# Sigmoid attention and a spatially gated MLP on one core: the 64-row tail of the spatial product as row tiles of two batches, with four accumulators open together

## Chip, cores, metric

One core of one Trainium2 chip. The metric is the device time of one execution in microseconds (us); the kernel before took 665.77 us (median of 3 runs, 665.56 to 666.07). Below, PE is TensorE's matmul stream, PEld its weight loads, DVE is VectorE, ACT ScalarE, POOL GpSimd, SP the queue that issues most DMAs.

## The reference, cut to what matters

```python
# q, k, v: (8 batches, 12 heads, 448 tokens, 64); all fp32
attn = sigmoid(q @ k.T / 8 - log(448)); x = (attn @ v) as (8, 448, 768)
h = relu(x @ w_in)                      # 768 -> 1024
u, v = h[..., :512], h[..., 512:]
v_n = (v - mean(v)) / sqrt(var(v) + 1e-6)
v_s = einsum('ts,bsd->btd', w_spatial, v_n) + b_spatial   # the spatial product, 448 x 448
out = (u * v_s) @ w_out                 # 512 -> 768
```

## The kernel before, in words

Batches are worked in four rounds of two (`m` = 0 to 3; an even batch `b0`, an odd one `b1`). A round is `attention(m)`, then `gate_values` for seven token tiles in groups (0,1), (2,3), (4,5), (6), then the spatial products, the gating by `u` and the output products, in an order that is written out by hand at the end of `attn_gmlp_kernel` (L690 to L713). `in_program_order` ties every engine to that order: whatever stands first in an engine's program waits first.

**Two-part numbers.** fp32 operands are split into a high and a low part in the type fp32r. `product` (L376) issues for each chunk of the contraction three matmuls, high-high, low-high and high-low (`TERMS`), all into one bank of PSUM.

**The spatial product.** 448 tokens are three chunks of 128 rows and a tail of 64. For one batch and one of four feature blocks `fc` of 128, `spatial` (L451) issues 3 x 3 matmuls for the full chunks and two for the tail: 11 of 448 columns, 352 in the whole kernel. The tails of both batches share the tile `vns[3]` ("the short tile"), whose two halves are filled so that `[:, 0]` holds the even batch's high part in rows 0 to 63 and its low part in rows 64 to 127, and `[:, 1]` the odd batch's low part in rows 0 to 63 and its high part in rows 64 to 127. The spatial weights of the tail stand in both halves of the rows. So the first tail matmul (times the weights' high part, 128 rows) gives high-high plus low-high at once, and the second (times the weights' low part, also 128 rows) gives high-low, and low-low with it.

**PSUM.** One pool `ps_2` of four buffers, each two banks, which is all of PSUM, serves every product (`banks`, L115): `pv` (gate values, L379 by way of `product`), `pg` (spatial), `pu` (the `u` half), `po` (output), `psc` and `pav` (attention). A new tile takes a buffer when the reader of that buffer's last tile is done. The four groups of `gate_values` fill all four just before the spatial products; their readers are the `relu` on ACT (L414).

**Round 0 also loads weights.** `load_weights(n)` runs n steps of a generator that splits `w_in` and `w_out`: DVE (L126, L129, L132, L199, L215), ACT (L200, L205), SP (L158). `gate_values` calls it ahead of its `relu`, `spatial` (2 steps) ahead of the bias addition (L473), `gated` 2 steps ahead of L496 and 2 at its end. In rounds 1 to 3 the generator is empty.

**After the spatial products.** `spatial` ends with the DVE addition of the bias (L473) into a tile `g` of the three-buffer tag `tmp`. `gated` (L478) forms `pu`, multiplies (L496), and splits the result (L109 on ACT, L110 on DVE) for `output` (L512), which needs both halves of a batch. `start_loads(m + 1)` puts the next round's loads on SP.

Order of the products in a round: `pg` of b0 (two groups of two `fc`), `pu` of b0 (two), `pg` of b1 (two), `po` of b0 for the first third, `pu` of b1 (two), the rest of `po`.

Of the kernel before, what the change touches and what calls it, by code (L numbers as in the profile page):

```python
# [14 lines left out]
P = 128  # L15
# [20 lines left out]
def attn_gmlp_kernel(  # L36
# [25 lines left out]
    nc = tc.nc  # L62
    B, NHP, _, _ = qk.shape
    S = out.shape[3]
# [5 lines left out]
    HALF = 64  # L70
    NFULL = 3
# [24 lines left out]
    w_sp_s = const.tile([P, 4, 2, 512], F32R, name="w_sp_s")  # L96
    b_bc = const.tile([P, 512], F32, name="b_bc")
# [10 lines left out]
    def split(hi, lo, src, copy):  # L108
        copy(hi, src)  # L109
        nc.vector.tensor_sub(lo, src, hi.bitcast(F32))  # L110

    def banks(name):
        return ps_2.tile([P, 2, 512], F32, tag="ps2", name=name)
# [112 lines left out]
    def load_weights(n):  # L226
        for _ in range(n):
            next(weights, None)
# [22 lines left out]
    def attention_splits(b, hp, halfway=False):  # L251
        raw = loaded[b, hp][:, HALF:]
        s = work.tile([P, 2, 2 * S], F32R, tag="split", name=f"qks_{b}_{hp}", bufs=3)[:, :, :PART]
        (nc.vector.tensor_copy if b > 1 or halfway else nc.scalar.copy)(s[:, 0], raw)  # L254
        parts_of[b, hp] = s
        if not halfway:
            finish_splits(b, hp)
# [12 lines left out]
    TERMS = ((0, 0), (1, 0), (0, 1))  # L270
# [104 lines left out]
    def product(ps, pairs, more=()):  # L375

        ops = [(st(a), mv(c)) for st, mv in pairs for a, c in TERMS] + list(more)
        for i, (st, mv) in enumerate(ops):
            nc.tensor.matmul(ps, st, mv, start=i == 0, stop=i == len(ops) - 1)  # L379
# [10 lines left out]
    def half_of(w, o, k, n):  # L390

        block, col = divmod((o // 2 * n + k) * 2 + o % 2, 4)
        return w[:, block, :, col * P : (col + 1) * P]

    vns = {}
# [50 lines left out]
    def cols_of(b):  # L446
        return slice(0, S) if b % 2 else slice(512 - S, 512)

    gates = {}

    def spatial(b, fcs):  # L451

        odd = b % 2
        cols = cols_of(b)
        pg = banks(f"pg_{b}_{fcs[0]}")
        for i, fc in enumerate(fcs):
            fs = slice(fc * P, (fc + 1) * P)
            pairs = []
            for c in range(NFULL):
                vn = vns[c + 4 if odd else c]  # L460
                pairs.append(
                    (lambda a, vn=vn: vn[:, a, fs], lambda p, c=c: w_sp_s[:, c, p, cols])
                )

            short = vns[NFULL][:, odd, fs]
            product(
                pg[:, i, :S], pairs, [(short, w_sp_s[:, NFULL, a, cols]) for a in range(2)]
            )
        load_weights(2)
        g = work.tile([P, 2, 512], F32, tag="tmp", name=f"g_{b}_{fcs[0]}", bufs=3)[:, :, :S]  # L470
        bb = b_bc[:, cols]
        bb = bass.AP(bb.tensor, bb.offset, [list(bb.ap[0]), [0, 2], list(bb.ap[1])])
        nc.vector.tensor_add(g, pg[:, :, :S], bb)  # L473
        gates[b, fcs] = g

    hidden = {}
# [1 line left out]
    def gated(b, fcs):  # L478

        odd = b % 2  # L480
        g = gates.pop((b, fcs))
        pu = banks(f"pu_{b}_{fcs[0]}")
        for i, fc in enumerate(fcs):
            fs = slice(fc * P, (fc + 1) * P)
            product(
                pu[:, i, :S],
                [
                    (
                        lambda a, cc=cc: half_of(w_u[0], fc, cc, NCC)[:, a],
                        lambda c, cc=cc: x_s[:, c, cc, odd * S : (odd + 1) * S],  # L490
                    )
                    for cc in range(NCC)
                ],
            )
        load_weights(2)
        nc.vector.scalar_tensor_tensor(g, pu[:, :, :S], 0.0, g, op0=ALU.max, op1=ALU.mult)  # L496
        if odd:
            gs = [
                work.tile([P, 2, 512], F32R, tag="big", name=f"gs_{b}_{fcs[0]}_{a}", bufs=BIG)[:, :, :S]
                for a in range(2)  # L500
            ]
        else:
            gs = work.tile([P, 2, 2 * S], F32R, tag="split", name=f"gs_{b}_{fcs[0]}", bufs=3)
            gs = [gs[:, a].rearrange("p (i s) -> p i s", i=2) for a in range(2)]
        split(gs[0], gs[1], g, nc.scalar.copy)
        for i, fc in enumerate(fcs):
            hidden[b, fc] = [part[:, i] for part in gs]
        load_weights(2)

    def output(b, es, final=False):  # L510

        osb = work.tile([P, 2, 512], F32, tag="tmp", name=f"osb_{b}_{es[0]}", bufs=3)[:, :, :S]  # L512
        if final:

            pos = [banks(f"po_{b}_{e}")[:, 0, :S] for e in es]
        else:
            po = banks(f"po_{b}_{es[0]}")
            pos = [po[:, i, :S] for i in range(2)]
        for i, e in enumerate(es):
            product(  # L520
                pos[i],
                [
                    (
                        lambda a, fc=fc: half_of(w_out_s, e, fc, NFC)[:, a],
                        lambda c, fc=fc: hidden[b, fc][c],
                    )
                    for fc in range(NFC)
                ],
            )
            if final:  # L530
                h = S // 2
                nc.scalar.copy(osb[:, i], pos[i])  # L532
                nc.sync.dma_start(out[b, e, :, h:], osb[:, i, h:])
                nc.scalar.dma_start(out[b, e, :, :h], osb[:, i, :h])
        if final:
            return
        nc.scalar.copy(osb, po[:, :, :S])  # L537
        nc.sync.dma_start(out[b, es[0] : es[0] + 2].rearrange("e p s -> p e s"), osb)
# [7 lines left out]
    def start_loads(m):  # L546
        n = m * 2 * NHP
        ahead(attention_loads, n)
        ahead(attention_loads, n + 1)
        ahead(value_loads, n)  # L550
        ahead(attention_loads, n + 2)
        ahead(attention_loads, n + 3)
        if m:
            ahead(value_loads, n + 2)
# [85 lines left out]
    def attention(m):  # L640

        if m:
            attention_by_fours(m)
            return
        end = 2 * NHP
        ats = {}

        def scores(n, ts):
            for t in ts:
                ats[n, t] = attention_scores(*units[n], t)  # L650

        short, evens, odds = (NFULL,), tuple(range(NFULL)), tuple(range(NFULL + 1, TILES))
        full = evens + odds
        for n in (0, 2):
            if not n:
                first_splits(*units[0])
            if n:
                scores(n, short + evens)
            else:
                scores(n, evens)  # L660

            def loads():
                ahead(value_loads, n + 2, end)
                ahead(attention_loads, n + 4, end)
                ahead(attention_loads, n + 5, end)

            if n:
                loads()
            scores(n, odds)
            if not n:  # L670
                scores(n, short)
            for t in full:
                if copied(*units[n], t):
                    sigmoid(ats[n, t], ats[n, t])
            if not n:
                loads()
            load_weights(3 if n else 2)
            for i in range(3 if n else 2):
                attention_splits(*units[n + 2 + i])
            if not n:  # L680
                load_weights(1)
            attention_values(*units[n], lambda t: ats.pop((n, t)), direct=n)
        attention_by_fours(0)
        w_u.append(const.tile([P, NCC, 2, F], F32R, tag="w_u", name="w_u_s"))
# [4 lines left out]
    pairs = [(0, 1), (2, 3)]  # L689
    for m in range(B // 2):  # L690
        attention(m)
        for ts in ((0, 1), (2, 3), (4, 5), (6,)):
            gate_values(m, ts)
        b0, b1 = 2 * m, 2 * m + 1
        more = m < B // 2 - 1
        for fcs in pairs:
            spatial(b0, fcs)
        for fcs in pairs:
            gated(b0, fcs)
        for fcs in pairs:  # L700
            spatial(b1, fcs)
        start_loads(m + 1)
        output(b0, (0, 1))
        for fcs in pairs:
            gated(b1, fcs)
        output(b0, (2, 3))
        output(b0, (4, 5))
        if more:
            for n in range(3):
                attention_splits(*units[(m + 1) * 2 * NHP + n])  # L710
        output(b1, (0, 1))
        output(b1, (2, 3))
        output(b1, (4, 5), final=not more)  # L713
# [55 lines left out]
```

## Time and profile before

| | |
|---|---|
| median of 3 runs | 665.77 us (665.56 to 666.07) |
| profiled execution: its own time, its span | 666.02 us, 664.2 us |
| PE busy | 659.2 us, 99% of the span, 3830 matmuls |
| DVE, ACT, POOL busy | 318.0, 250.1, 18.5 us |
| granted TensorE clock, mean | 1.0 |

How to read it: busy shares say how much an engine worked, the view of waits says which engine stood still and for whom, the chain says what followed what up to the end, and the timeline gives start and length of each run of like instructions. The end of a matmul is modelled, so rates are taken from starts, not from lengths.

### The profile page before, as it was taken

What the parts mean: (1) busy time and instruction counts of PE and PEld (TensorE: products, weight loads), DVE (VectorE), ACT (ScalarE), POOL (GpSimd) and SP (SyncE); (2) the same over time, 40 slices, a digit from 0 to 9 for tenths busy, and PEclk for the clock granted to TensorE, in tenths of its full rate; (3) what the DMA queues carried; (4) which work ended last, traced back from release to release, by engine and by line L of the source; (5) the groups of instructions that cost most, each with busy time, mean ns of one, the idle gap of its engine ahead of it and who ended that gap; (6) DMA issues with size and microseconds to landing.
All of it is one profiled execution on the core that took longest, in us unless ns stands there. A gap on an engine that the chain in (4) does not pass through costs nothing.

```text
span 664.2 us, 8979 instructions
## 1 busy us (share of the span) xinstructions
PE 659.2 (99%) x3830; PEld 510.1 (77%) x3830; DVE 318.0 (48%) x464; ACT 250.1 (38%) x283; POOL 18.5 (3%) x36
## 2 busy tenths in 40 slices
PE   9999999999999999999999999999999999999997
PEld 3655889999765588999966558899986655899997
DVE  4989888852545237223156515721315741653110
ACT  5986322411766510011187641010127872101011
POOL 0000010000000002000000001100000000110000
PEclk9999999999999999999999999999999999999999
DMA  8755213432431310000344050000024510000003
GB/s 298 238 179 188 63 37 94 136 122 83 169 140 58 137 60 0 1 29 0 112 141 169 29 178 18 1 1 28 29 84 142 169 56 1 1 1 0 29 29 111
DMA packets 20695, 55.75 MB, mean 84 GB/s; under 512 B 1968, under 2 KB 8496, under 8 KB 20656
## 3 DMA queue, kind: packets, MB, share of 16 engines
q1 hardware_dynamic: 20368, 54.96, 24.2%
q8 instruction: 30, 0.49, 0.3%
q10 hardware_dynamic: 288, 0.23, 0.1%
q14 instruction: 9, 0.07, 0.0%
HBM read 44.17 MB, written 11.01 MB: 83 GB/s over the span
## 4 chain that ended last, share of the span: by engine, by line
PE 99%; ACT 0%; DVE 0%; issue 0%
PE pav L346 20%; PE pu L379 17%; PE po L379 17%; PE pv L379 17%; PE psc L311 14%; PE pg L379 11%; PE psc L293 3%; PE warm L388 0%; ACT osb L532 0%; DVE zeros L384 0%; DVE bias_s L100 0%; DVE mhalf L102 0%
## 5 line engine op out<-in xcount | busy, mean ns | idle before, releaser
L275 ACT ACTIVATE at<-psc,bias_s 128x896 f32<-128x896 f32 x129 | 120.4, 1009 | 6.1 <-PE psc L311 4.6
L346 PE MATMUL pav<-at,v 128*64 128x448 f32 (+1 forms) x684 | 120.1, 544 | 0.0
L379 PE MATMUL pu<-x_s,w_u_s 128*128 128x448 f32 x576 | 116.5, 362 | 0.0
L379 PE MATMUL po<-gs,w_out_s 128*128 128x448 f32 x576 | 116.5, 362 | 0.0
L379 PE MATMUL pv<-w_g_s,x_s 128*128 128x512 f32 x504 | 115.4, 390 | 0.0
L379 PEld LDWEIGHTS pu<-x_s,w_u_s 128*128 128x128 f32 x576 | 108.0, 188 | 7.2
L379 PEld LDWEIGHTS po<-gs,w_out_s 128*128 128x128 f32 x576 | 108.0, 187 | 7.3
L379 PEld LDWEIGHTS pv<-w_g_s,x_s 128*128 128x128 f32 x504 | 94.3, 188 | 22.3 <-PE pav L346 2.8
L346 PEld LDWEIGHTS pav<-at,v 128*64 128x64 f32 (+1 forms) x684 | 41.7, 136 | 70.8 <-issue 64.0
L311 PEld LDWEIGHTS psc<-qks 64*128 64x128 f32 x840 | 77.9, 185 | 14.8 <-DVE x_s L110 5.2
L311 PE MATMUL psc<-qks 64*128 64x448 f32 x840 | 88.6, 365 | 0.0
L379 PE MATMUL pg<-w_sp_s,vn 128*128 128x448 f32 x352 | 71.7, 362 | 0.0
L379 PEld LDWEIGHTS pg<-w_sp_s,vn 128*128 128x128 f32 x352 | 66.0, 187 | 4.7
L109 ACT CAST gs<-g 128x896 fp32r<-128x896 f32 x16 | 15.1, 942 | 120.3 <-DVE g L496 120.3
L537 ACT COPY osb<-po 128x896 f32<-128x896 f32 x23 | 20.9, 908 | 104.1 <-PE po L379 104.1
L110 DVE TENSOR_TENSOR x_s<-pav,x_s 128x896 fp32r<-128x896 f32 x16 | 17.1, 1089 | 81.5 <-ACT x_s L109 81.5
L496 DVE SCALAR_TENSOR_TENSOR g<-pu,g 128x896 f32<-128x896 f32 x16 | 17.5, 1091 | 80.1 <-PE pu L379 80.1
L261 DVE TENSOR_TENSOR qks<-raw,qks 128x848 fp32r<-128x848 f32 x46 | 47.4, 1039 | 1.1 <-ACT qks L254 0.2
L414 ACT ACTIVATE rv<-pv 128x1024 f32<-128x1024 f32 (+1 forms) x16 | 14.7, 919 | 75.9 <-PE pv L379 75.9
L418 DVE BATCH_NORM_STATS2 stats<-rv 128x6 f32<-128x512 f32 x28 | 19.0, 679 | 38.9 <-ACT rv L414 38.9
L109 ACT CAST x_s<-pav 128x896 fp32r<-128x896 f32 x16 | 14.1, 909 | 53.9 <-PE pav L346 53.9
L591 DVE COPY wval_s<-psc 128x896 f32<-128x896 f32 x9 | 9.8, 1092 | 47.3 <-PE psc L311 47.3
(59 smaller groups left out, 368.7 us busy)
## 6 DMA issues: line engine op xcount, KB each, us to landing
raw<-qk_dram SPq DMA_DIRECT2D x47, 456.0 KB, 5.1
v<-v_dram SPq DMA_DIRECT2D x24, 448.0 KB, 3.6
out_dram<-osb SPq DMA_DIRECT2D x23, 448.0 KB, 2.6
wraw<-w_in_dram SPq DMA_DIRECT2D x12, 512.0 KB, 6.2
wraw<-w_out_dram SPq DMA_DIRECT2D x6, 512.0 KB, 3.4
wraw<-w_sp_dram SPq DMA_DIRECT2D x4, 256.0 KB, 6.2
raw<-qk_dram SPq DMA_DIRECT2D x1, 296.0 KB, 2.9
b_bc<-b_sp_dram SPq DMA_DIRECT2D x1, 256.0 KB, 6.6
```

Source lines behind the costliest of these rows:

```text
L109: copy(hi, src)
L110: nc.vector.tensor_sub(lo, src, hi.bitcast(F32))
L261: nc.vector.tensor_sub(s[:, 1], loaded[b, hp][:, HALF:], s[:, 0].bitcast(F32))
L275: nc.scalar.activation(at, src, AF.Sigmoid, bias=bias_s, scale=QK)
L293: nc.tensor.matmul(psc[odd * HALF : (odd + 1) * HALF, j, :S], raw[rows, :HALF], raw[rows, HALF + Q :], start=True, stop=True,)
L311: nc.tensor.matmul(psc[:, j, :S], st[rows, k : k + P], mv[rows, Q:PART], start=i == 0, stop=i == len(ops) - 1,)
L346: nc.tensor.matmul(pav[heads, odd, :S], vt[rows, t, heads], at[rows, j], start=start, stop=t == NFULL,)
L379: nc.tensor.matmul(ps, st, mv, start=i == 0, stop=i == len(ops) - 1)
L414: nc.scalar.activation(rv[:, :n], pv[:, :n], AF.Relu)
L418: nc.vector.bn_stats(stats, rv[:, i])
L496: nc.vector.scalar_tensor_tensor(g, pu[:, :, :S], 0.0, g, op0=ALU.max, op1=ALU.mult)
L537: nc.scalar.copy(osb, po[:, :, :S])
```

## The change

The eight spatial accumulators of a round (two batches, four `fc`, in four two-bank tiles) are opened together. The second tail matmul of each is replaced by one on 64 rows alone, which holds the high part, so that high-low is formed and low-low no longer; the even batch's uses rows 0 to 63 and the odd batch's rows 64 to 127, and the two are issued one behind the other into different banks. All eight of a round stand in `spatial_shorts`, behind the first `spatial` group. The order of the round becomes: `pg` b0 first half, the eight short ones, `pg` b0 second half, `pg` b1 (two), `pu` b0 (two), `pu` b1 first, `start_loads`, `po` b0 first third, `pu` b1 second, the rest of `po`. The bias additions are issued after their accumulators end; that of the last tile stands behind `gated(b0, ...)`'s first group.

```diff
+    def spatial_room(b, fcs):
+        pgs[b, fcs] = banks(f"pg_{b}_{fcs[0]}")
+    def spatial_shorts(m, groups):
+        for fcs in groups:
+            for i, fc in enumerate(fcs):
+                for odd in range(2):
+                    b = 2 * m + odd
+                    rows = slice(odd * HALF, (odd + 1) * HALF)
+                    nc.tensor.matmul(
+                        pgs[b, fcs][:, i, :S],
+                        vns[NFULL][rows, odd, fc * P : (fc + 1) * P],
+                        w_sp_s[rows, NFULL, 1, cols_of(b)],
+                        start=(b, fcs) not in begun,
+                        stop=(b, fcs) in begun,
+                    )
+            begun.update((2 * m + odd, fcs) for odd in range(2))
...
     def spatial(b, fcs):
-        pg = banks(f"pg_{b}_{fcs[0]}")
+        pg = pgs[b, fcs]
...
-            product(
-                pg[:, i, :S], pairs, [(short, w_sp_s[:, NFULL, a, cols]) for a in range(2)]
-            )
+            ops.append((vns[NFULL][:, b % 2, fs], w_sp_s[:, NFULL, 0, cols]))
+            ended = (b, fcs) in begun
+            for n, (st, mv) in enumerate(ops):
+                nc.tensor.matmul(pg[:, i, :S], st, mv,
+                    start=n == 0 and not ended, stop=n == len(ops) - 1 and ended)
+        begun.add((b, fcs))
         load_weights(2)
+    def biased(b, fcs):
...
-        nc.vector.tensor_add(g, pg[:, :, :S], bb)
+        nc.vector.tensor_add(g, pgs.pop((b, fcs))[:, :, :S], bb)
...
-        for fcs in pairs:
-            spatial(b0, fcs)
-        for fcs in pairs:
-            gated(b0, fcs)
-        for fcs in pairs:
-            spatial(b1, fcs)
+        for b in (b0, b1):
+            for fcs in pairs:
+                spatial_room(b, fcs)
+                if (b, fcs) == (b0, pairs[0]):
+                    spatial(b, fcs)
+        spatial_shorts(m, pairs)
+        biased(b0, pairs[0])
+        for b, fcs in ((b0, pairs[1]), (b1, pairs[0])):
+            spatial(b, fcs)
+            biased(b, fcs)
+        spatial(b1, pairs[1])
+        gated(b0, pairs[0])
+        biased(b1, pairs[1])
+        gated(b0, pairs[1])
+        gated(b1, pairs[0])
         start_loads(m + 1)
         output(b0, (0, 1))
-        for fcs in pairs:
-            gated(b1, fcs)
+        gated(b1, pairs[1])
```

## Rows read from the trace of the kernel before

**Rows 1.** The profile's page, two lines: busy time by engine (us, share of the span, instructions), and the chain that ended last, by engine.

```profile
PE 659.2 (99%) x3830; PEld 510.1 (77%) x3830; DVE 318.0 (48%) x464; ACT 250.1 (38%) x283; POOL 18.5 (3%) x36
PE 99%; ACT 0%; DVE 0%; issue 0%
```

**Rows 2.** The view of waits, PE alone: who waited for whom, total us, times, longest.

```profile
PE warm L388 <- DVE zeros L384: 1.2, 1, 1.2
```

**Rows 3.** The chain in order of time (start us, us, what): the spatial products, the `u` products and the next ones of round 0, and a block of 36 score pairs of round 2.

```profile
95.07 8.81 PE pg L379 x44
103.88 14.41 PE pu L379 x72
...
335.37 7.40 PE psc L311 x72
```

**Rows 4.** Timeline of PE, one row from each of four short stretches at 335 us (start us, us, what, count): the last four-tile matmuls of 64x64, then the first pairs of 64-row matmuls (64*128 is rows times columns of the stationary).

```profile
334.82 0.56 PE L293 MATMUL psc<-raw 64*64 64x448 f32 x4
335.30 0.47 PE L311 MATMUL psc<-qks 64*128 64x448 f32 x2
335.62 0.56 PE L311 MATMUL psc<-qks 64*128 64x448 f32 x4
335.82 0.56 PE L311 MATMUL psc<-qks 64*128 64x448 f32 x4
```

**Rows 5.** The same view at 333 us: a 128-row output product is followed by 64x64 tiles.

```profile
333.15 0.56 PE L379 MATMUL po<-gs,w_out_s 128*128 128x448 f32 x2
333.35 0.36 PE L379 MATMUL po<-gs,w_out_s 128*128 128x448 f32 x1
333.64 0.61 PE L293 MATMUL psc<-raw 64*64 64x448 f32 x4
334.06 0.56 PE L293 MATMUL psc<-raw 64*64 64x448 f32 x4
```

**Rows 6.** The same view at 342 us: 64-row pairs are followed by pairs of 128 rows and 64 columns.

```profile
342.42 0.36 PE L311 MATMUL psc<-qks 64*128 64x448 f32 x2
342.71 0.60 PE L346 MATMUL pav<-at,v 128*64 128x448 f32 x2
343.13 0.92 PE L346 MATMUL pav<-at,v 128*64 128x448 f32 x4
```

**Rows 7.** The same view at 392 us: 64x64 tiles are followed by full 128x128 matmuls.

```profile
392.57 0.54 PE L346 MATMUL pav<-at,v 64*64 64x448 f32 x2
393.04 0.50 PE L379 MATMUL pv<-w_g_s,x_s 128*128 128x512 f32 x1
393.38 0.63 PE L379 MATMUL pv<-w_g_s,x_s 128*128 128x512 f32 x2
393.61 0.62 PE L379 MATMUL pv<-w_g_s,x_s 128*128 128x512 f32 x2
```

**Rows 8.** Timeline of round 0 around the start of the spatial products, PE, then ACT, then one DVE row (brackets: idle before, and releaser).

```profile
94.91 8.97 PE L379 MATMUL pg<-w_sp_s,vn 128*128 128x448 f32 x44
...
98.31 0.62 ACT L205 CAST w_u_s<-wval_s 128x512 fp32r<-128x512 f32 x1 [3.87 <-DVE wval_s L132]
101.54 0.68 ACT L200 ACTIVATE wraw<-wraw 128x512 f32<-128x512 f32 x1 [2.60 <-DVE wraw L199]
102.11 0.59 ACT L414 ACTIVATE rv<-pv 128x512 f32<-128x512 f32 x1
...
101.02 0.43 DVE L199 TENSOR_SCALAR wraw<-wraw 128x512 f32<-128x512 f32 x1
```

**Rows 9.** The chain at the start of the kernel: the step from a DVE memset to the first matmul that waited for it.

```profile
0.91 0.28 DVE zeros L384
1.19 0.05 issue
```

**Rows 10.** Timeline of round 1: PE's spatial products, and the same `relu` on ACT.

```profile
258.32 8.97 PE L379 MATMUL pg<-w_sp_s,vn 128*128 128x448 f32 x44
...
258.57 0.60 ACT L414 ACTIVATE rv<-pv 128x512 f32<-128x512 f32 x1 [3.10 <-PE pv L379]
```

**Rows 11.** Timeline of DVE: the last write of token tile 6 (L436) in round 0 and in round 1.

```profile
105.47 0.75 DVE L436 SCALAR_TENSOR_TENSOR vn<-rv,rstd,vn 128x512 fp32r<-128x512 f32 x1
...
263.68 0.75 DVE L436 SCALAR_TENSOR_TENSOR vn<-rv,rstd,vn 128x512 fp32r<-128x512 f32 x1
```

**Rows 12.** Timeline of DVE in round 0 behind that: weight steps (first rows of two runs of them), bias additions, the gating and its split.

```profile
106.13 0.69 DVE L129 SCALAR_TENSOR_TENSOR wval_s<-wraw,wval_s 128x512 uint32<-128x512 uint32 x1
...
108.86 1.09 DVE L473 TENSOR_TENSOR g<-pg,b_bc 128x896 f32<-128x896 f32 x1
109.86 0.68 DVE L129 SCALAR_TENSOR_TENSOR wval_s<-wraw,wval_s 128x512 uint32<-128x512 uint32 x1
...
112.59 1.09 DVE L473 TENSOR_TENSOR g<-pg,b_bc 128x896 f32<-128x896 f32 x1
...
116.31 1.08 DVE L496 SCALAR_TENSOR_TENSOR g<-pu,g 128x896 f32<-128x896 f32 x1
118.40 1.09 DVE L110 TENSOR_TENSOR gs<-g,gs 128x896 fp32r<-128x896 f32 x1 [1.01 <-ACT gs L109]
119.41 0.69 DVE L129 SCALAR_TENSOR_TENSOR wval_s<-wraw,wval_s 128x512 uint32<-128x512 uint32 x1
```

**Rows 13.** Timeline of SP in round 0: the next round's loads, then the outputs.

```profile
123.64 6.15 SPq L241 DMA_DIRECT2D raw<-qk_dram  x2
...
137.31 34.37 SPq L538 DMA_DIRECT2D out_dram<-osb  x6
```

**Rows 14.** Timeline of PE at the start: the first matmuls of 512 columns, and the first two pairs of 64 rows that follow one another at the later rate.

```profile
1.23 2.74 PE L388 MATMUL warm<-zeros 128*128 128x512 bf16 x6 [1.23 <-DVE zeros L384]
...
5.94 0.66 PE L311 MATMUL psc<-qks 64*128 64x448 f32 x4
```

More of the change, by code (lines that the diff above doesn't have):

```diff
@@ L449, in attn_gmlp_kernel @@
     gates = {}
+    pgs = {}
+    def spatial_room(b, fcs):
[14 more added lines that the diff above has]
+            begun.update((2 * m + odd, fcs) for odd in range(2))
@@ L451, in spatial @@
+    begun = set()
     def spatial(b, fcs):
-        odd = b % 2
         cols = cols_of(b)
-        pg = banks(f"pg_{b}_{fcs[0]}")
+        pg = pgs[b, fcs]
         for i, fc in enumerate(fcs):
             fs = slice(fc * P, (fc + 1) * P)
[L458 to L462, printed above, removed]
-                )
-            short = vns[NFULL][:, odd, fs]
-            product(
-                pg[:, i, :S], pairs, [(short, w_sp_s[:, NFULL, a, cols]) for a in range(2)]
-            )
+            ops = [
+                (vns[c + 4 if b % 2 else c][:, a, fs], w_sp_s[:, c, p, cols])
+                for c in range(NFULL)
+                for a, p in TERMS
+            ]
+            ops.append((vns[NFULL][:, b % 2, fs], w_sp_s[:, NFULL, 0, cols]))
+            ended = (b, fcs) in begun
+            for n, (st, mv) in enumerate(ops):
+                nc.tensor.matmul(
+                    pg[:, i, :S],
+                    st,
+                    mv,
+                    start=n == 0 and not ended,
+                    stop=n == len(ops) - 1 and ended,
+                )
+        begun.add((b, fcs))
@@ L469, in spatial @@
         load_weights(2)
+    def biased(b, fcs):
         g = work.tile([P, 2, 512], F32, tag="tmp", name=f"g_{b}_{fcs[0]}", bufs=3)[:, :, :S]
-        bb = b_bc[:, cols]
+        bb = b_bc[:, cols_of(b)]
         bb = bass.AP(bb.tensor, bb.offset, [list(bb.ap[0]), [0, 2], list(bb.ap[1])])
-        nc.vector.tensor_add(g, pg[:, :, :S], bb)
+        nc.vector.tensor_add(g, pgs.pop((b, fcs))[:, :, :S], bb)
         gates[b, fcs] = g
```

## The prediction

> **What bounds the kernel now.** The page comes first: PE is busy for 659.2 of 664.2 us and is 99% of the chain that ended last [rows 1]. The view of waits comes second: PE waits once in the whole execution, 1.2 us at the start [rows 2]. So every TensorE slot that goes is time won, and every wait that PE is given is time lost, with nothing downstream to absorb it. Third come rates, from the chain and from starts in the timeline: 44 spatial matmuls in 8.81 us and 72 of `u` in 14.41 us make 0.200 us for one of 448 columns [rows 3].
>
> **Part 1: slots removed.** A round has eight high-low tail matmuls, 8 x 0.200 = 1.60 us. Now each has 64 rows, and two run at once if they lie in different row halves and banks. The attention scores have that very shape: successive pairs start at 335.62 and 335.82, so a pair takes one slot of 0.20 [rows 4]. Four pairs are 0.80 us; 0.80 us a round is saved, 3.2 us in four rounds.
>
> **Part 2: two changes of tile shape a round.** The short pairs stand between full 128x128 matmuls, so PE goes to 64-row tiles and back, 8 times in all. The trace has neither change, but both their ends, in starts:
> - Leaving 128x128 for 64x64: 333.35 to 333.64 is 0.29 where a slot is 0.20, so 0.09 lost [rows 5].
> - The first 64x128 pair after another shape holds up the second: 335.30 to 335.62 is 0.32 against 0.20, so 0.12 (two decimals; over the block, 7.40 us for 36 pairs is 0.20 above 36 x 0.200, both losses together [rows 3, 4]).
> - Leaving 64x128: 342.42 to 342.71 is 0.29, again 0.09; the 64-column shape behind it loses less at its second start, 0.42 (342.71 to 343.13) where the steady step of such tiles is 0.38 (two of them from 334.06 to 334.82), so 0.04 to 0.05 [rows 4 to 6].
> - Entering 128x128: 393.04 to 393.38 is 0.34 where the next step is 0.23, so 0.11 [rows 7].
>
> In: 0.09 + 0.11 = 0.20. Out: 0.09 + 0.11 = 0.20. I take 0.40 us a round, 1.6 us in all; the nearest rows bound a change by 0.14 (rows 5 and 6 with their cheaper second halves) and 0.22, so 1.1 to 1.8 us. Parts 1 and 2 leave a saving of 3.2 - 1.6 = 1.6 us (1.4 to 2.1).
>
> The Trainium skill, page "TensorEngine Tiling (Array Packing)", section "Key Properties", says that a change of tiling mode, unlike a change of tile, drains the engine. The rows agree, with 0.20 us for each. A sum that follows the same page's section "Theoretical Speedup" alone, up to twice for a contraction of 64, would keep all of the 3.2 us.
>
> **Part 3: the wait for the fourth accumulator, round 0.** The pool has four buffers, and the short pairs of the second group need all four, so one is the buffer of the last gate product (token tile 6), free only when its `relu` on ACT is done. Before, the first two spatial tiles took older buffers and this one was needed from 103.7 on. In round 0 that `relu` is late: on ACT it stands behind a weight step (L200, 101.54), which waits for DVE (L199, 101.02), and runs from 102.11 to 102.70 [rows 8]. Nothing in front of it is touched by the change. PE's new times: the first spatial group starts at 94.91 and has 20 matmuls, so it ends at 98.91; pairs start at 99.00 and 99.32; the even half of the third at 99.52; its odd half, which is the first to write the fourth buffer, waits until 102.70 plus about 0.05 for the hand-over (0.05 of issue between a DVE memset and its matmul [rows 9]), 102.75. The refilled array again spends some 0.31 to the last pair (the 0.20 + 0.11 above), 103.06, and 0.30 to the first full matmul, 103.36. Without the wait that would be 99.72 + 0.30 = 100.02. Cost: 3.3 us. Bounds: 3.2 (nothing but the delay from 99.52 to 102.75) and 3.7 (if the fourth buffer falls to the first pair and all four come after 102.75).
>
> Behind PE's waiting matmul stands all of its program; DVE and ACT go on. In rounds 1 to 3 there are no weight steps: the `relu` starts 0.25 us after the first spatial matmul and ends at 259.17, while the third pair would come about 4.6 us after 258.32, at 262.9 [rows 10]. No wait there.
>
> **Part 4: what moved.** The odd batch's spatial products follow the even batch's directly, so token tile 6 is needed earlier. Round 0: the second group runs 103.36 to 107.5, and tile 6 is wanted at the seventh matmul of the next, 108.7; DVE wrote it by 106.22 [rows 11]: covered by 2.5 us, but only because PE waited before. Round 1: wanted at 268.7, there at 264.43. Zero.
>
> Round 0's DVE queue is nearly gapless behind this: two weight steps take 2.73 us (106.13 to 108.86), a bias addition 1.0, gating 1.08, the wait for ACT 1.01, the split 1.0 [rows 12]. Laid out in the new order, each group of `spatial` or `gated` brings its weight steps along: bias additions end at 109.9, 113.6 and 117.3, the first gating starts at 122.8 (PE ends that product at 122.7, 7.2 us after the spatial ones), the fourth bias addition ends at 129.6, the second gating starts at 132.3, its split ends at 135.4. PE ends the spatial products at 103.36 + 0.1 + 60 x 0.200 = 115.5, and wants the fourth accumulator's buffer and both splits for `po` three `u` groups later, at 115.5 + 3 x 7.2 = 137.1. Margins 7.5 and 1.7 us: zero, the second one thin. In rounds 1 to 3 `pu` of b1 covers that split (3.2 us of DVE and ACT work under 7.2 us of PE). The fourth `g` waits for the first one's buffer, which is the order on DVE anyhow. `start_loads` passes one `gated` in the program, and on SP still stands ahead of the outputs, with the weight loads ahead of it as before; SP is held by the weights' buffers until about the same step, and the loads ran at 123.64, 47 us before the next round [rows 13]. Zero. Fewer rows in the low product cost and save nothing else.
>
> **Sum.** -3.2 + 1.6 + 3.3 = +1.7 us. The profiled execution took 666.02 (span 664.2 and 1.8 around it), so 667.7; the median is 0.25 below that execution, so 667.5. Bounds: 3.2 - 2.1 = +1.1 to 3.7 - 1.4 = +2.3, or 666.9 to 668.1. About 0.2% (1.33 us) is what a measurement of this kernel can tell from no change; the forecast is 0.26% slower.
>
> **Rivals.**
> - **The buffer wait is not there or is much shorter, and PE runs through** (the other side). It decides from a `relu` of tile 6 that ends before 99.5 in round 0. For it: only that the row is one execution. Against: the queue that delays it is upstream of the change. Then -1.6, but the next things are late: tile 6 is wanted at 105.3 and there at 106.2 (0.9), and the output product at 133.8 finds a split that ends at 135.4, 1.6 in all with the 0.9 within it. That gives 665.8; with the DVE train shorter too, 664.2.
> - **The clock.** PE's array stands still for some 2.9 us (99.88, the end of the last half pair, to 102.75) in a kernel that else never pauses. At the start PE is at the low level, 1.2 GHz: six matmuls of 512 columns at 0.43 each, and two pairs 0.29 apart only from 5.94 [rows 14]. If the pause drops it, the price is at most half of such a stretch: (6.1 - 1.2) / 2 = 2.4 us, so 669.9, or half that for a shorter one, 668.7. Against: PE worked at the full level for 90 us before. The trace has no pause of this kind inside. The Trainium skill, "TensorE: Matmul & The Clock Gate", section "What's actually happening", says that the slow state is the default and that activity releases it; no run here shows whether this pause is enough to lose it.
> - **A change of shape costs less than in the rows**, down to nothing. Then 665.9. Against: every change in the trace shows it.
> - **The thin margin breaks**: round 0's DVE train falls behind and the output product waits 1 to 2 us more: 668.5 to 669.5.
>
> **Numbers.** Forecast 0.70; clock 0.13; no buffer wait 0.07 (0.04 of it faster by over 0.2%, the rest same); cheap shape change 0.05 (same); thin margin 0.05. Slower by over 0.2% means above 667.1: 0.13 + 0.05 and 0.64 of the forecast's 0.70, whose lower bound lies below it: 0.82. Within: 0.03 + 0.05 + 0.06 = 0.14. Faster: 0.04. The range 666.7 to 669.6 holds the forecast's bounds with the run's scatter, most of the clock case and of the thin margin, and leaves out the two cases below, about 0.12, and the full clock price.
>
> **What would show it.** Right: 80 full `pg` matmuls and 4 pairs a round where 88 full ones stood; PE's view of waits with one new entry, about 3.2 us, for ACT at L414, in round 0 only; gaps of 0.29 and 0.31 at both ends of the pairs in every round; rounds 1 to 3 shorter by 0.4 us each. Wrong: no such wait, pairs starting 0.2 apart in a row of eight, rounds 1 to 3 longer, a wait of `po` on L110 in round 0, or matmuls 0.4 apart behind the pause.

## The result, and the profile after

The changed kernel takes 669.7 us (median of 6 runs, 666.78 to 670.69), the kernel before in the same comparison 665.5 us (665.0 to 666.07): ratio 1.0056, 95% interval 1.0036 to 1.0075, so slower by 0.56% (the two medians alone would make 1.0063). The side is the one forecast. The range on record, 666.7 to 669.6, is met only at its upper end: 1.0056 times the 665.77 of the prediction is 669.5, and the median itself lies 0.1 us above the range. The point, 667.5, is 2.2 us too low, and the sum's own bounds, 666.9 to 668.1, do not hold the result. Runs of the changed kernel scatter over 3.9 us, those of before over 1.1 us, and the scatter goes with the clock: of eight executions the two at a mean granted clock of 0.999 took 666.8 and 667.5 us, the six at 0.994 to 0.997 took 669.1 to 670.7.

The traced execution is one of the two short ones: 666.78 us, span 665.0. Its page and its waits of PE, to be set against [rows 1, 2]:

```profile
PE 657.2 (99%) x3830; PEld 506.0 (76%) x3830; DVE 318.0 (48%) x464; ACT 249.9 (38%) x283; POOL 18.5 (3%) x36
PE 95%; DVE 3%; ACT 1%; issue 0%; ACTq 0%
```

```profile
PE pg L463 <- ACT rv L414: 2.8, 1, 2.8
PE warm L388 <- DVE zeros L384: 1.2, 1, 1.2
```

PE is busy 2 us less, and it waits once more: 2.8 us, in the new short matmuls, for the `relu` of a gate product. DVE and ACT, which had no part in the chain [rows 1], now have 4% of it. Where, the chain in order of time shows (start us, us, what), round 0:

```profile
100.01 0.44 DVE wraw L199
...
101.09 0.59 ACT rv L414
101.68 0.04 issue
101.72 0.67 PE pg L463 x3
102.39 12.21 PE pg L488 x60
```

and the timeline of PE over the same stretch (start us, us, what, count, idle before and releaser), answering to the first of [rows 8]:

```profile
93.90 4.17 PE L488 MATMUL pg<-w_sp_s,vn 128*128 128x448 f32 x20
98.00 0.87 PE L463 MATMUL pg<-w_sp_s,vn 64*128 64x448 f32 x5
101.72 0.67 PE L463 MATMUL pg<-w_sp_s,vn 64*128 64x448 f32 x3 [2.85 <-ACT rv L414]
102.32 12.28 PE L488 MATMUL pg<-w_sp_s,vn 128*128 128x448 f32 x60
136.04 4.96 PE L379 MATMUL po<-gs,w_out_s 128*128 128x448 f32 x24
```

Five short matmuls run, the sixth (the first to write the fourth accumulator) stands until 101.72, 0.04 us after the `relu` ended; the `relu` stood behind the weight step that waited for DVE's L199. In rounds 1 to 3 the same eight run through. Round 1 and the start of round 2 in the chain, first of the kernel before, then of the changed one:

```profile
229.70 28.79 PE pv L379 x126
...
393.11 7.03 PE pv L379 x30
```

```profile
231.62 28.79 PE pv L379 x126
260.40 4.01 PE pg L488 x20
264.41 1.01 PE pg L463 x8
265.43 12.21 PE pg L488 x60
...
394.64 28.79 PE pv L379 x126
```

A round, from the first gate product to that of the next, was 163.41 us and is 163.02: 0.39 saved. The eight short matmuls, four pairs and both changes of shape take 1.02 us (264.41 to 265.43) and 0.20 of the step behind it (12.21 us for 60 matmuls, where 60 x 0.200 are 12.01).

**Where the time went in this execution.** PE reached the first gate product 1.0 us earlier than in the trace before (the first spatial matmul is at 93.90, not 94.91). The traces of this case put that point up to 1.7 us apart with no change ahead of it, and 0.9 us of the difference is there within the first 10 us (the first matmuls of L293 start at 8.97 and at 9.86 in the chain), so this is an accident of the start. Round 0 is 2.92 us longer (by the starts of its and the next round's first gate products in the timeline, 65.18 to 231.54, against 66.19 to 229.63): 3.3 for the pause less 0.39 saved. Three rounds save 0.35 to 0.39 each. -1.0 + 2.9 - 1.1 = +0.8, as 666.78 stands to 666.02. The median has something on top that this execution lacks: the clock.

### The profile page after: what moved, and what is told of

It is laid out like the page before. It is cut to its first block, busy times and chain, and to the rows that moved or that the text cites. A ratio compares the mean times of both kernels' runs of the same rounds, so it can differ in the third digit from the quotient of the medians.

```text
span 665.0 us, 8983 instructions
## 1 busy us (share of the span) xinstructions
PE 657.2 (99%) x3830; PEld 506.0 (76%) x3830; DVE 318.0 (48%) x464; ACT 249.9 (38%) x283; POOL 18.5 (3%) x36
## 4 chain that ended last, share of the span: by engine, by line
PE 95%; DVE 3%; ACT 1%; issue 0%; ACTq 0%
PE pav L346 20%; PE po L379 17%; PE pu L379 17%; PE pv L379 14%; PE psc L311 14%; PE pg L488 9%; PE psc L293 3%; DVE vn L436 1%; DVE stats L418 1%; PE pg L463 1%; ACT rv L414 1%; DVE vn L435 0%; PE warm L388 0%; DVE rv L424 0%; DVE wval_s L132 0%
## 5 line engine op out<-in xcount | busy, mean ns | idle before, releaser
L488 PE MATMUL pg<-w_sp_s,vn 128*128 128x448 f32 x320 | 65.8, 363 | 0.0
L488 PEld LDWEIGHTS pg<-w_sp_s,vn 128*128 128x128 f32 x320 | 59.7, 187 | 5.4 <-issue 1.2
```

The costliest lines, as they stand in the source:

```text
L488: nc.tensor.matmul(pg[:, i, :S], st, mv, start=n == 0 and not ended, stop=n == len(ops) - 1 and ended,)
```

## Experiments

Each kernel is the changed one with the edit shown. "The clock fell" means a run with a mean granted clock of 0.997 or less; all kernels without a pause had 0.999 or 1.000.

**1. The changed kernel again**, to trace an execution of the common sort.

> The changed kernel once more. Its own runs so far scatter from 666.8 to 670.7 us, and the lower a run's mean granted clock, the longer it is (0.999 at 666.8 and 667.5, 0.994 at 670.7); the traced one is among the shortest. Theory A (the pause of 2.9 us in round 0 lets the clock fall in most executions): if this trace has a mean clock of 0.997 or less, its matmuls start 0.4 us apart for a stretch directly behind the pause at about 102 us and nowhere else, rounds 1 to 3 keep 163.0 us each, and the time is 669 to 671. Theory B (the extra time comes from the 64-row pairs, in every round): the low clock stands behind the pairs of rounds 1 to 3 too, and those rounds are longer than 163.0.

668.82 us, ratio 1.0043 (1.0029 to 1.0056); the clock fell in three of four runs, the traced one (668.66, clock 0.997) among them. Busy time by stretch (us: PE, PEld, DVE, ACT, POOL, granted clock, DMA share, GB/s), then two short stretches of PE's timeline behind the pause:

```profile
98.00:102.00 4.00, 1.15 (x9) 0.49 (x7) 3.27 (x7) 1.34 (x3) 0.00 (x0) 1.00 0.44 131
102.00:106.00 4.00, 4.00 (x13) 3.33 (x14) 3.11 (x6) 0.00 (x0) 1.10 (x2) 0.61 0.00 0
106.00:110.00 4.00, 4.00 (x21) 3.72 (x20) 3.90 (x8) 1.31 (x2) 0.00 (x0) 0.96 0.41 130
110.00:118.00 8.00, 8.00 (x42) 7.49 (x41) 7.86 (x14) 2.61 (x4) 0.00 (x0) 1.00 0.43 133
```

```profile
103.64 0.95 PE L488 MATMUL pg<-w_sp_s,vn 128*128 128x448 f32 x2
...
106.70 0.76 PE L488 MATMUL pg<-w_sp_s,vn 128*128 128x448 f32 x3
```

PE is "busy" for all of 102 to 106, but with 13 matmuls in 4 us where 20 belong: the granted clock is 0.61 there, so the lower level (1.2 GHz) for most of it: in finer stretches the granted clock is 0.50 from 102.90 to 106.31. Two matmuls take 0.95 there (0.37 from start to start), three take 0.76 after it (0.20). Round 0 is 167.95 us against 166.36 in the trace without a fall: 1.6 us for 3.4 us at half clock. Rounds 1 and 2 are 163.03 each, with the same pairs and no fall. Theory A holds but for its time: 669 to 671 was expected, the traced run took 668.66.

**2. The same order without row tiles.**

```diff
-                    rows = slice(odd * HALF, (odd + 1) * HALF)
+                    rows = slice(0, P)
```

> The changed kernel's order and its four open accumulators, but the eight tail matmuls of a round on all 128 rows, so low-low is formed as before and no row tiles are left. Theory A: the pause stays (the fourth buffer is wanted at the sixth of the eight, about 1.0 us behind the first spatial group instead of 0.6, so 2.8 us of wait and about 2.9 lost), there is no change of tile shape, rounds 1 to 3 are 163.4 us as before, and the clock falls in most executions as with the change: 668.4 where it holds, 670.5 to 672 where it falls, median some 671, scatter over 2 us. Theory B: no row tiles, so no fall: 668.4 with a scatter under 1 us.

669.12 us (668.58 to 670.19), ratio 1.0053 (1.0040 to 1.0067). The order and the four open accumulators alone make the kernel slower, with no row tile in it:

```profile
PE pg L463 <- ACT rv L414: 2.6, 1, 2.6
```

Its rounds 1 and 2 are 163.41 us, as before, so the 0.39 is the pairs'. But the clock fell in one of five runs, not in most: that part of theory A missed here. The traced run, without a fall, also waited 0.8 us for a load near its start, ahead of anything that was changed.

**3. The pause taken away on ACT.** `gate_values` for token tile 6 does its weight step behind the `relu`.

```diff
-        load_weights(1 if ts[0] else 5)
+        last = ts[0] == 2 * NFULL
+        if not last:
+            load_weights(1 if ts[0] else 5)
...
         nc.scalar.activation(rv[:, :n], pv[:, :n], AF.Relu)
+        if last:
+            load_weights(1)
```

> The changed kernel with one order turned round: for token tile 6 the weight step comes behind the relu, not ahead of it, so that on ACT the relu no longer waits for DVE. Row tiles and order of the products stay. Theory A: the relu ends at about 99.5 on the clock of the trace before, when the third pair is due, so the pause shrinks from 2.85 to 0 to 0.2 us; what shows up next is token tile 6 (wanted 105.3, there 105.6: 0.2 to 0.3 us) and the output product behind the second split (0.5 to 1.0 us). No fall of the clock: all runs at 1.000, scatter 1 us as before. 665.5 - 1.6 + 1.0 = 664.9 us (664.2 to 665.5), faster than before by 0.1%. Theory B: the pairs still bring the clock down, 668 and more, scatter as with the change.

664.39 us (11 runs, 663.35 to 665.16), ratio 0.9979 (0.9970 to 0.9988): faster than before. The clock is 0.999 or 1.000 in all eleven. ACT and PE in round 0:

```profile
99.39 0.59 ACT L416 ACTIVATE rv<-pv 128x512 f32<-128x512 f32 x1
102.03 0.69 ACT L200 ACTIVATE wraw<-wraw 128x512 f32<-128x512 f32 x1 [2.05 <-DVE wraw L199]
```

```profile
95.46 4.17 PE L492 MATMUL pg<-w_sp_s,vn 128*128 128x448 f32 x20
99.56 1.14 PE L467 MATMUL pg<-w_sp_s,vn 64*128 64x448 f32 x8
100.64 12.30 PE L492 MATMUL pg<-w_sp_s,vn 128*128 128x448 f32 x60
```

The eight run through in 1.08 us. The waits that I expected behind the relu did not come in this execution: round 0 takes 163.15 us, rounds 1 and 2 take 163.02 and 163.05. (It is the slowest of the eleven, with a wait of 1.3 us for a load near its start.) Row tiles without the pause gain; theory B is out.

**4. The pause taken away on PE**, with four changes of shape a round in place of two.

```diff
-        spatial_shorts(m, pairs)
+        spatial_shorts(m, pairs[:1])
         biased(b0, pairs[0])
...
+        spatial(b0, pairs[1])
+        spatial_shorts(m, pairs[1:])
```

> The changed kernel with the eight short matmuls in two places: four behind the first spatial group, four behind the second. The fourth buffer is then wanted some 4.6 us later, behind the relu, so the pause goes without touching ACT; but there are four changes of tile shape a round in place of two. Theory A with 0.20 us for a change: rounds 1 to 3 go back from 163.0 to 163.4 us, nothing saved in them; round 0 has no pause for the relu and no wait for token tile 6, and waits about 1.0 to 1.5 us for the split ahead of the output product. Clock 1.000 in all runs. 665.5 + 0 + 1.3 = 666.8 us (665.4 to 667.2). If a change of shape cost nothing, rounds would stay at 162.2 in both kernels, and this one would come out at 663.5 to 664.5. Theory B: clock as low as with the change.

666.32 us (11 runs), ratio 1.0009 (1.0000 to 1.0018); no clock fell. The chain in round 1:

```profile
258.04 4.01 PE pg L488 x20
262.05 0.60 PE pg L463 x4
262.66 4.21 PE pg L488 x20
266.87 0.61 PE pg L463 x4
267.48 8.21 PE pg L488 x40
```

The 20 full matmuls behind the first group of pairs take 4.21, not 4.01, and the 40 behind the second 8.21. Rounds 1 and 2 are 163.45 us, 0.42 more than with two changes: 0.21 for one. That is all that the pairs had saved. Round 0 waited 0.4 us for token tile 6, which I had put at zero, and not for the split ahead of the output product, where I had put 1.0 to 1.5. The view of waits does not list it, the chain of round 0 does:

```profile
104.55 0.76 DVE vn L436
105.32 0.04 issue
105.36 6.88 PE pg L488 x33
```

**5. What the pairs cost in all.** Experiment 3 without the short matmuls (the output lacks the high-low term of the tail):

```diff
-                    stop=n == len(ops) - 1 and ended,
+                    stop=n == len(ops) - 1,
...
-        spatial_shorts(m, pairs)
```

> The version with the relu first, and the eight high-low tail matmuls of a round left out: no short pairs, no change of tile shape, and the output lacks that term. It prices the pairs: rounds 1 to 3 fall from 163.03 to 163.41 - 8 x 0.200 = 161.81 us if a full matmul is worth 0.200 and four pairs with two changes of shape cost 4 x 0.20 + 0.41 = 1.21. If the pairs cost more than 0.20 each and a change less, the sum with split_shorts (0.42 for two more changes) does not close.

Rounds 1 and 2 are 161.81 us each, 659.78 us in all (one run). So eight full tail matmuls are 163.41 - 161.81 = 1.60, and the pairs with two changes 163.03 - 161.81 = 1.22: 0.42 by experiment 4 for the changes, 0.80 is left for four pairs, which is the 4 x 0.20 that was expected. The sum closes.

**6. How long a pause brings the clock down.** Five kernels were to move the length of the pause. The first two swap the groups, with pairs and with full rows:

```diff
-        spatial_shorts(m, pairs)
+        spatial_shorts(m, pairs[::-1])
```

> The changed kernel with the two groups of short pairs in the other order, so that the fourth buffer is wanted by the first pair and PE stands still for about 3.4 us in round 0 in place of 2.85. The traced pause of the change let the clock fall in 9 of 12 runs, for one stretch of 3.41 us that cost 1.6 us in round 0 of the trace that has it; full rows with a pause of 2.65 us let it fall in 1 of 5. Theory A1 (the length of the pause decides): the clock falls in all runs, 0.997 or less; 3.7 us for the pause, 665.6 - 1.6 + 3.7 = 667.7 without a fall, 669.3 with one stretch, 671 with two. Theory A2 (64-row pairs around the pause decide): as with the change, some runs at 0.999 and above.

> The same swap with the tail matmuls on all 128 rows: no row tiles, a pause of about 3.3 us. Theory A1 (length of the pause): the clock falls in all or nearly all runs, 665.6 + 3.7 = 669.3 without a fall and 670.9 or more with one, so a median of 670.9. Theory A2 (the 64-row pairs): it falls in 1 of 5 or so as in the unswapped full rows, median 669.3, clock 0.999 to 1.000.

669.84 and 669.96 us (ratios 1.0061 and 1.0060). They failed as experiments on length: the sixth short matmul waited in either order, 2.84 and 2.65 us as unswapped. The four buffers went to the accumulators in the order in which these were first written, not in which they were named, so the last one was wanted at the sixth short matmul again. So these kernels are repeats, and as such they count: the clock fell in five of five runs with pairs, four of five with full rows. In the trace with pairs the granted clock falls within the pause and stays low longer:

```profile
98.00:102.00 4.00, 1.16 (x8) 0.77 (x8) 3.27 (x7) 1.15 (x2) 0.00 (x0) 0.82 0.47 131
102.00:106.00 4.00, 4.00 (x12) 3.11 (x11) 3.08 (x7) 0.00 (x0) 1.10 (x2) 0.50 0.00 0
106.00:110.00 4.00, 4.00 (x18) 3.67 (x17) 3.93 (x7) 1.30 (x2) 0.00 (x0) 0.82 0.45 131
```

It is low (0.50) from 100.60 to 107.42, 6.8 us of which 1.1 lie in the pause, and round 0 is 168.97 us: 2.6 more than without a fall.

The next two put the first `fc` of both groups first (`for i` outside `for fcs`), so that the fourth short matmul waits; the fifth kernel puts the pairs into the middle of the second group:

```diff
+        spatial(b0, pairs[1], (0,))
         spatial_shorts(m, pairs)
         biased(b0, pairs[0])
...
+        spatial(b0, pairs[1], (1,))
```

> The earlier swap of groups moved nothing, because a buffer falls to the accumulator that is written first, so that the sixth short matmul waited in either order. Here the first fc of both groups goes first, so that the last buffer is first written by the fourth short matmul: a pause of 3.05 us in place of 2.85. Theory A: 0.2 us more for the pause, and the clock falls at least as often as with the change (14 of 17 runs so far): median 669 to 671; without a fall 667.7.

> The same on all 128 rows, a pause of 3.05 us in place of 2.65 and no row tiles. If the length of the pause decides how often the clock falls, it falls as often as with the pairs at 3.05 us (nearly always), median 670.5 to 671.5, 669.0 without a fall; if the half-empty array around the pause decides, it falls less often than with the pairs, as the full rows at 2.65 us did (1 of 5 and 4 of 5 on two chips).

> The changed kernel with the eight short matmuls 2.0 us later, in the middle of the second spatial group: the fourth buffer is wanted 2.0 us later and the pause in round 0 shrinks from 2.85 to 0.85 us; still two changes of shape a round, ACT and DVE in the old order. Theory A: a pause is paid at its length, 1.3 us with the hand-over, and this one is too short to bring the clock down: 665.7 - 1.6 + 1.3 = 665.4 us (664.8 to 665.8), all clocks 0.999 or above, rounds 1 to 3 at 163.03. If the clock falls at this pause too, 667 and 0.997.

Their waits of PE, in the order pairs early, full rows early, half a group later:

```profile
PE pg L464 <- ACT rv L414: 3.0, 1, 3.0
```

```profile
PE pg L464 <- ACT rv L414: 3.1, 1, 3.1
```

```profile
PE pg L463 <- ACT rv L414: 0.8, 1, 0.8
```

| pause in round 0 (us) | tail matmuls | clock fell in | mean clock where it fell | median us |
|---|---|---|---|---|
| 0 (experiments 3, 4, 7) | pairs | 0 of 32 runs | | 664.39, 666.32, 664.08 |
| 0.8 (half later) | pairs | 0 of 11 | | 665.35 |
| 2.65 (full rows, and swapped) | full | 5 of 10 | 0.996 to 0.997 | 669.12, 669.96 |
| 2.85 (the change, again, swapped) | pairs | 14 of 17 | 0.994 to 0.997 | 669.7, 668.82, 669.84 |
| 3.05 (early) | pairs | 5 of 5 | 0.994 to 0.997 | 669.92 |
| 3.06 (early) | full | 4 of 5 | 0.997 | 670.63 |

The short pause costs its length and the refilling behind it, and no fall: round 0 is 164.34 us, 1.3 above rounds 1 and 2, and the kernel takes 665.35, expected 665.4. With the pairs a pause of 2.85 us costs 3.3 in the same way, and pauses of 2.65 to 3.06 us brought, in 28 of 37 runs, a fall on top. The runs of 0.8 and of 3.05 us come from one chip and one comparison: 0 of 11 there against 9 of 10. Between 2.65 and 3.06 us the length does not settle it alone: full rows at 2.65 fell in 1 of 5 runs on one chip and in 4 of 5 on another, and at 3.05 on one chip the pairs' runs go down to 0.994 where the full rows' stay at 0.997.

The other three traces with a fall have it too. Full rows swapped, pairs early and full rows early, each over the stretch in which the granted clock is 0.50 (columns as above):

```profile
101.78:105.18 3.40, 2.89 (x8) 2.59 (x9) 2.02 (x5) 0.46 (x1) 1.10 (x2) 0.50 0.00 0
102.30:109.12 6.82, 6.63 (x19) 5.48 (x20) 5.69 (x11) 1.45 (x3) 1.10 (x2) 0.50 0.12 23
103.60:107.00 3.40, 3.40 (x11) 3.02 (x10) 2.55 (x6) 0.00 (x0) 0.71 (x2) 0.50 0.00 0
```

PE's waits end at 102.29, 102.49 and 102.24 there. So the fall began inside the pause in three of five traces and up to 1.4 us behind it in two. It lasted 3.4 us in three and 6.8 in two, both of these with pairs.

**7. A version to beat both.** Weight steps that PE does not need at once come later:

```diff
-        load_weights(1 if ts[0] else 5)
+        last = ts[0] == 2 * NFULL
+        if not last:
+            load_weights(1 if ts[0] else 5)
...
             vns[t] = vn
+        if last:
+            load_weights(1)
...
-        load_weights(2)
         nc.vector.scalar_tensor_tensor(g, pu[:, :, :S], 0.0, g, op0=ALU.max, op1=ALU.mult)
...
-        load_weights(2)
+        load_weights(4)
```

> A version meant to beat both: the changed kernel, with round 0's weight step of token tile 6 behind its last write (not only behind its relu), and the weight steps of gated behind its split in place of ahead of the gating, so that DVE serves PE first. PE should wait nowhere after its first matmuls in any execution: 665.6 - 1.6 = 664.0 us (663.5 to 664.5), all clocks 0.999 or above. If the relu's place alone is what counts, it equals the version with the relu first (664.4).

664.08 us (10 runs, 663.44 to 664.53), ratio 0.9975 (0.9966 to 0.9984), no clock fell. It is faster than the kernel before and than the changed one. Its gain over experiment 3 (0.3 us between medians, in different comparisons) is within what these measurements can tell.

## Why the prediction was right, and where it was off

- **What bounds: right.** PE waited nowhere, so removed slots and added waits both showed in full.
- **Part 1, 0.80 us a round: right.** 1.60 for the full tail matmuls less 0.80 for four pairs (experiment 5).
- **Part 2, 0.40 us a round: right.** 0.42 for two changes of shape (experiment 4), though none of the trace's rows had this very pair of shapes; the rounds save 0.39, as 0.80 - 0.40 said. The page "TensorEngine Tiling (Array Packing)" of the Trainium skill, "Key Properties", gives the rule that a change of mode drains TensorE and no price. The traces agree in that every change costs time, 0.21 us each; here two of them are half of what the pairs win.
- **Part 3, 3.3 us in round 0: right to the place and the size.** The wait is at the first write of the fourth accumulator, for the `relu` behind L200; PE goes on 0.04 us after it, and round 0 lost 166.36 - 163.44 + 0.39 = 3.3 us. (The view of waits was to show about 3.2 and shows 2.8: it counts from the end of the matmul before, the forecast from the start at which the sixth was due.) Runs without a fall, 666.8, 667.2 and 667.5, stand 1.6 us above the median of before; the sum said 1.7.
- **Part 4: the zeros held, one margin was misjudged.** The margin of 1.7 us ahead of the output product was counted to its first matmul. That product takes the second half of the features only at its seventh matmul, 1.2 us later. In the changed kernel the split ends at 134.56, and PE has begun the product at 136.04 and needs it at 137.2:

```profile
133.47 1.09 DVE L110 TENSOR_TENSOR gs<-g,gs 128x896 fp32r<-128x896 f32 x1 [1.01 <-ACT gs L109]
```

  For the same reason experiments 3 and 4 were expected too slow there. Without the pause nothing of DVE's train waits long: the rival without a buffer wait was put at 665.8, and experiment 3, which is that case, gave 664.4.
- **The numbers: the step that failed is the choice of the likeliest case.** The sum has no term for the clock, and the clock rival was given 0.13 against 0.70 for a pause without a fall. The clock fell in 14 of 17 runs, and the median's +4.2 us is the 1.6 of the runs without a fall and 2.6 more, which is what the fall cost in the trace with pairs swapped. The rival's price came near: 669.9 with a full stretch and 668.7 with half of one were forecast; runs with a fall took 668.3 to 670.7. That is in part luck. The price was half of the 4.9 us of slow matmuls at the start, for which the granted clock reads 1.00 (1 to 6 us of the trace before), while the low stretches behind the pause last 3.4 or 6.8 us; and it was to be 2.4 at most, while the trace with pairs swapped paid 2.6. That the result falls at the edge of the range is luck too: the range was drawn to leave out the full clock price, 669.9, and the median, 669.7, came out beside that. What spoke against the clock rival, 90 us of work at the full level ahead of the pause, did not protect the kernel. The trace before had no pause inside and so could not tell; that is where the doubt should have been larger. The Trainium skill, "TensorE: Matmul & The Clock Gate", "What's actually happening", has the slow state as the default that activity lifts; the traces here show it coming back in or behind a single pause of under 3 us (2.85 with the pairs, 2.65 with full rows).

## What to carry to other kernels

Where PE runs without a gap, opening more accumulators at once is a change of order: find the last reader of the buffer that each of them takes over, in the round where that reader's engine is busiest, before counting the slots won. Row tiles of 64 win a slot for each pair and pay about 0.2 us at each change of shape, so gather them, and in one place. Move work that PE does not wait for behind the read that frees PSUM on the queue that does it: here one weight step behind one `relu` turned 0.56% slower into 0.2% faster.

## What the runs showed of the hardware that was not expected

- A single pause of 2.65 to 3.06 us in 665 us of otherwise almost unbroken matmuls brought the granted clock to its lower level in 28 of 37 runs, one of 0.8 us in none of 11. The fall showed at different places in the traces, inside the pause (100.60, wait until 101.69) or 0.3 us after the full matmuls had begun again (102.90), and lasted 3.4 or 6.8 us; the price in round 0 was 1.6 us in a trace of the first length and 2.6 in one of the second.
- The busy share of PE hides it: in the stretch at 0.61 of the clock PE is busy for 4.00 of 4.00 us. The count of matmuls (13 against 20) and the granted clock show it.
- What decides whether it falls, and for how long, stays open. Over the table longer pauses fell more often (5 of 10, 14 of 17, 9 of 10), but the chips were not the same across it, and one chip against another moved the first of these from 1 of 5 to 4 of 5. At equal pauses the runs with 64-row pairs had the lower clocks, on one chip and in five runs each.
- The granted clock does not show every slow stretch: at the start of the trace before it reads 1.00 while bf16 matmuls of 512 columns start some 0.43 us apart ([rows 14]); those of 512 columns at 393 us start 0.23 apart ([rows 7]). So the level at the start is read from rates alone.
